# Moving the transposes and small products of a weight fold by half steps, and converting six weight tiles ahead of the loop instead of four

## The chip, the cores and the metric

The kernel runs on one core of a Trainium2 chip. The metric is the time of one execution on the device in microseconds (us). The engines are named as in the profile: PE is TensorE (PEld its weight loads), DVE is VectorE, ACT is ScalarE, POOL is GpSimd and SP is SyncE, which here only issues DMA transfers. Each engine runs its own instructions in order, so an instruction that waits holds up everything behind it on the same engine.

## The reference

Three layers follow one another, on 3072 tokens of 384 values. The first is a gated linear attention, whose state decays by alpha; the second a dense layer with the activation `h * sigmoid(h)`; the third a mixture of eight experts, of which each token takes the two with the largest noisy logits.

```
x = _attn_ref(q, k, v, alpha)            # B=4, H=8, S=768, D=48 -> 3072 x 384
h = x @ w_in                             # 384 x 2048, w_in is float64
x = (h / (1 + exp(-h))) @ w_out          # 2048 x 384, w_out is float64
logits = x @ w_gate + log1p(exp(x @ w_noise)) * noise
top2 = the two largest of 8, softmax over them
out[token] += weight * (relu(x @ w1[e]) @ w2[e])
```

The float64 weights of the dense layer matter here: `w_in` and `w_out` come as pairs of 32-bit words, which the kernel itself turns into float32, and then into a high and a low part (`win_h`, `win_l`, `wo_h`, `wo_l`) so that three passes on TensorE (high by high, high by low, low by high) give float32 accuracy.

## The kernel before

**Steps.** The tokens are cut into `NB = 8` blocks of `BT = 384`, each of three chunks of 128. For each block `j` and each of the `MF = 16` slices `m` of the hidden width there is one step, so 128 steps, numbered `i = 16 * j + m`. In a step, `l1(j, m)` multiplies a slice of `w_in` into a PSUM bank `ph` (nine matmuls, L474), `act1` makes the activation of it (`th` on ACT, `gf` on DVE, `gh` on ACT, `gl` on DVE), and `l2` (nine matmuls, L501) multiplies the result of two steps ago (`LAG = 2`) with a slice of `w_out` into the three banks `acc`. There are two `ph` banks, so `l1` of a step needs `gf` of two steps before to have read its bank. Each step also runs one `unit()` of the attention of a later chunk. Five units make a chunk: `u = 0` scans P on DVE and makes the score products (L247), `u = 1` scans R on DVE and makes the state (L264, then L272 and L273 on DVE), `u = 2` and `u = 3` make the output (L286, L290), `u = 4` transposes it into `xh` and `xl`. The first 15 units (three chunks) run ahead of the loop; this is the prologue. The other seven blocks and the experts run nothing of what is changed here.

**Weight tiles.** `w_in` and `w_out` come in 32 tiles, in the order i0, i1, i2, o0, i3, o1, i4, o2 and so on (i for `w_in`, o for `w_out`). `conv()` takes the next one: `narrow` makes float32 of it with three DVE instructions (L148 to L150) into a buffer `f` of a ring of six (named `row` and `wf`), and then the raw words of the tile three places on are requested on SP's queue, into the buffer just read. ACT makes the high part (L374). The low part of an i tile comes from a DMA on POOL's queue that adds the high part to `f` (L379) and a copy on ACT (L380), that of an o tile from DVE (L377). Of an o tile, `fold` also transposes `f` on PE (L94, three blocks, copied by ACT as `ft`, L387), and `product` multiplies that with the gate weights `wgn` (six matmuls, L394), which gives 16 more columns of `w_out` (so `l2` writes the gate logits beside its output). `product` writes into free columns of the bank of the next `l1`. ACT reads them (`fp`, L396, then `wo_h`, L397), and DVE makes the low part (L398).

**The order.** It is written out by hand. `later(n, fn)` puts a piece off by `n` ticks, and `tick()` issues what is due. In the first block (`j = 0`) each step has two halves, each with a `conv()` and a `tick()`; the first takes an i tile and the second an o tile (called halves A and B, and their tiles narrow A and narrow B, below). So on DVE a step reads: narrow A, L377 of the o tile before, pieces of the attention, `gf`, narrow B, L398, `gl`, scans of the next chunk. Within the prologue four tiles are converted.

Of the kernel before, what the change touches and what calls it, by code (L numbers as in the profile page):

```python
# [8 lines left out]
F32 = mybir.dt.float32  # L9
# [4 lines left out]
AF = mybir.ActivationFunctionType  # L14
# [7 lines left out]
DM = H * D  # L22
DFF = 2048
E = 8
# [10 lines left out]
BT = 384  # L35
# [17 lines left out]
def attention_mlp_moe(ctx: ExitStack, tc: tile.TileContext, aqk, vt, win, wout, wgn, noise, w12,  # L53
# [3 lines left out]
    PE, DVE, ACT, POOL = nc.tensor, nc.vector, nc.scalar, nc.gpsimd  # L57
# [34 lines left out]
    def flip(o, x):  # L92
        n = x.shape[0]
        PE.transpose(o, x, ident[:n, :n])  # L94
# [25 lines left out]
    wo_l = wpool.tile([128, MF, LGN], F32R)  # L120
# [7 lines left out]
    def next_f():  # L128
        turn[0] += 1
        return ring[turn[0] % len(ring)]  # L130
# [16 lines left out]
    def narrow(t, f):  # L147
        DVE.tensor_scalar(f, t[:, :, 1], 3, 0x3fffffff, op0=OP.logical_shift_left, op1=OP.bitwise_and)  # L148
        DVE.scalar_tensor_tensor(f, t[:, :, 1], -0x40000000, f, op0=OP.bitwise_and, op1=OP.bitwise_or)
        DVE.scalar_tensor_tensor(f, t[:, :, 0], 29, f, op0=OP.logical_shift_right, op1=OP.bitwise_or)  # L150
        return f.bitcast(F32)
# [156 lines left out]
    dq, lazy, clock = [], [False], [0]  # L308

    def later(n, fn, pe=0):  # L310
        dq.append((clock[0] + n, pe, fn))
# [7 lines left out]
    def tick():  # L319
        clock[0] += 1  # L320
        due = [x for x in dq if x[0] <= clock[0]]
        dq[:] = [x for x in dq if x[0] > clock[0]]
        for *_, fn in sorted(due, key=lambda x: x[1]):
            fn()
# [26 lines left out]
    def unit():  # L351
        next(gen, None)
# [6 lines left out]
    def wl(n=1):  # L359
        for _ in range(n):  # L360
            if wloads:
                kind, m = wloads.pop(0)
                (load_win if kind == "i" else load_wout)(m)

    def conv():
        if not wpreps:
            return
        kind, m = k = wpreps.pop(0)
        f = next_f()
        narrow(raw.pop(k), f.bitcast(I32))  # L370
        wl()
        h, l = (win_h, win_l) if kind == "i" else (wo_h, wo_l)
        h, l = [x[:, m].rearrange("p k j -> p (k j)") if kind == "i" else x[:, m, :DM] for x in (h, l)]
        later(1, lambda: ACT.activation(h, f, AF.Copy, scale=-1.0))  # L374
        if kind == "o":
            later(1 + (not lazy[0]), lambda: fold(m, f), 1)
            later(2, lambda: DVE.scalar_tensor_tensor(l, f, -1.0, h.bitcast(F32), op0=OP.mult, op1=OP.subtract))  # L377
        else:
            later(1, lambda: POOL.dma_start(f, h.bitcast(F32), accum_op=OP.add), 2)  # L379
            later(5, lambda: ACT.activation(l, f, AF.Copy, scale=-1.0))  # L380

    def fold(m, f):
        p = p1.tile([128, KD, 128], F32, name="ps1")
        for k in range(KD):
            flip(p[:, k], f[:, k * 128:(k + 1) * 128])
        t = stg.tile([128, KD, 128], F32, name="ft", bufs=2)
        ACT.activation(t, p, AF.Copy)  # L387

        later(1, lambda: mids.append((m, t)))

    def product(p):
        m, t = mids.pop(0)
        for k in range(KD):
            PE.matmul(p, t[:, k], wgn_t[:, k], start=(k == 0), stop=(k == KD - 1))  # L394
        h, w = wo_h[:, m, DM:], stg.tile([128, 2 * E], F32, name="fp", bufs=1)
        later(1, lambda: ACT.activation(w, p, AF.Copy, scale=-1.0))  # L396
        later(1, lambda: ACT.activation(h, w, AF.Copy))  # L397
        later(2, lambda: DVE.tensor_sub(wo_l[:, m, DM:], w, h.bitcast(F32)))  # L398

    mids = []  # L400

# [8 lines left out]
    for i in range(3 * 5):  # L410
        unit()
        tick()
        if i in (0, 1, 6, 11):
            conv()
    lazy[0] = True

# [48 lines left out]

    def l1(j, m):
        p = pl.tile([128, 512], F32, name="ph")
        if mids:
            product(p[:, BT:BT + 2 * E])
        p = p[:, :BT]  # L470
        n = 0
        for k in range(KD):
            for w, x in ((win_h, XH[j]), (win_h, XL[j]), (win_l, XH[j])):
                PE.matmul(p, w[:, m, k], x[:, k], start=(n == 0), stop=(n == 3 * KD - 1))  # L474
                n += 1
        PH[j, m] = p

    def act1(j, m):
# [189 lines left out]
    for i in range(NS + LAG):  # L668
        if i < NS:
            j, m = divmod(i, MF)  # L670
            l1(j, m)
            if MF <= i < MF + E:
                init_rows(i - MF)
# [30 lines left out]
            if j == 0:  # L704
                conv()
                tick()
                if held:
                    step(held[0])
                    step(held[0])
                conv()  # L710
                tick()
                if held:
                    run(held.pop())
            else:
                if held:
                    run(held.pop())
                    while dq:
                        tick()
                    lazy[0] = False
                run(act1(j, m))  # L720
# [5 lines left out]
        if i >= LAG:  # L726
            j, m = divmod(i - LAG, MF)
# [87 lines left out]
    for i in range(NS + LAG):  # L815
        if i < NS:
            q, f = divmod(i, FF)
# [25 lines left out]
        if i >= LAG:  # L843
            q, f = divmod(i - LAG, FF)
# [16 lines left out]
    with tc.If(bad != 0), ExitStack() as fc:  # L861
# [8 lines left out]
        with tc.For_i(0, B, 1) as b, tc.For_i(0, NP, 1) as pr:  # L870
            for s in range(2):
                av, qv, kv = [fw.tile([D, NCB, C], F32, name=f"f{x}") for x in "aqk"]
                for n, t in enumerate((av, qv, kv)):
                    o, w = (1, CP) if n == 0 else (AL + (n - 1) * NP * C, C)
# [8 lines left out]
                for x in range(2):  # L883
                    p = pl.tile([128, 512], F32, name="ph")
# [3 lines left out]
                for e in range(D):  # L888
                    u = fw.tile([D, S], F32, name="fu")
                    w = fw.tile([D, S], F32, name="fs")  # L890
                    for x in range(2):
                        h = slice(x * HS, (x + 1) * HS)
                        p = pl.tile([128, 512], F32, name="ph")
# [14 lines left out]
        for src, dst in ((win, wt[0]), (wout, wt[1])):  # L908
            for m in range(MF):
                t = fw.tile([128, DM, 2], I32, name="fraw")  # L910
                nc.sync.dma_start(t.rearrange("p n w -> p (n w)"), src[m])
                f = narrow(t, fw.tile([128, DM], I32, name="wf"))
# [6 lines left out]
        with tc.For_i(0, B, 1) as b, tc.For_i(0, NCB, 1) as c:  # L919
# [5 lines left out]
            for m in range(MF):  # L925
                p = pl.tile([128, 512], F32, name="ph")
# [9 lines left out]
            p = fps.tile([128, KD, C], F32, name="ft")  # L936
# [3 lines left out]
            p = fps.tile([128, 2 * E], F32, name="fl")  # L940
# [9 lines left out]
            for e in range(E):  # L950
                w = fw.tile([128, W3N], F32, name="fw3")
                nc.sync.dma_start(w, w12[e])
                p2 = pa.tile([128, 512], F32, name=f"acc{1 + e % 2}")
                for f in range(FF):
                    p = pl.tile([128, 512], F32, name="ph")
# [3 lines left out]
                    h = fw.tile([128, C], F32, name="fh")  # L959
# [75 lines left out]
```

## Time and profile before

| | us |
|---|---|
| three runs | 1086.50, 1091.56, 1091.65 (median 1091.56) |
| profiled execution | 1086.38 |
| its span from first to last instruction | 1084.5 |
| PE busy | 1044.5 (96%) |
| DVE busy | 591.6 (55%) |
| ACT busy | 400.7 (37%) |
| POOL busy | 225.4 (21%) |

The span is 1.9 us shorter than the execution's time; what lies around it is not in the trace. Shares of the whole span say little by themselves here, since the stages differ: PE is at work without a gap in most of the span, and in the first 140 us it is not.

### The profile page before, as it was taken

What the parts mean: (1) busy time and instruction counts of PE and PEld (TensorE: products, weight loads), DVE (VectorE), ACT (ScalarE), POOL (GpSimd) and SP (SyncE); (2) the same over time, 40 slices, a digit from 0 to 9 for tenths busy, and PEclk for the clock granted to TensorE, in tenths of its full rate; (3) what the DMA queues carried; (4) which work ended last, traced back from release to release, by engine and by line L of the source; (5) the groups of instructions that cost most, each with busy time, mean ns of one, the idle gap of its engine ahead of it and who ended that gap; (6) DMA issues with size and microseconds to landing.
All of it is one profiled execution on the core that took longest, in us unless ns stands there. A gap on an engine that the chain in (4) does not pass through costs nothing. (4 is left out here: it accounts for less than half of the span.)

```text
span 1084.5 us, 16739 instructions
## 1 busy us (share of the span) xinstructions
PE 1044.5 (96%) x6323; PEld 1012.1 (93%) x6323; DVE 591.6 (55%) x1369; ACT 400.7 (37%) x869; POOL 225.4 (21%) x223
## 2 busy tenths in 40 slices
PE   5987799999999999999999999999999999999997
PEld 4877799999999999999999998999999999999997
DVE  6787956657778687775737552244333333324221
ACT  3344443334333433334344332244333333323221
POOL 4121201310313003130010132211212122221203
PEclk9988899999999999999999999999999999999999
DMA  8465661445424324240033342445444344353204
GB/s 222 124 164 169 154 204 60 133 148 186 123 78 145 100 79 129 85 138 18 1 103 108 117 139 30 114 106 155 112 96 118 86 95 107 68 121 77 47 10 54
DMA packets 53577, 117.16 MB, mean 108 GB/s; under 512 B 6768, under 2 KB 31856, under 8 KB 53488
## 3 DMA queue, kind: packets, MB, share of 16 engines
q1 hardware_dynamic: 39312, 90.99, 28.0%
q0 software_dynamic: 13760, 24.43, 12.3%
q8 instruction: 52, 0.85, 0.3%
q10 hardware_dynamic: 416, 0.58, 0.2%
q14 instruction: 37, 0.30, 0.1%
HBM read 82.22 MB, written 30.61 MB: 104 GB/s over the span
## 5 line engine op out<-in xcount | busy, mean ns | idle before, releaser
L784 PE MATMUL acc<-w3h,hx 128*128 128x384 f32 x832 | 241.1, 341 | 1.2 <-ACT y L794 1.2
L765 DVE SCALAR_TENSOR_TENSOR hx<-ph,hx 128x64 fp32r<-128x64 f32 (+1 forms) x192 | 79.1, 442 | 293.2 <-ACT hx L761 293.2
L796 POOL DMA_INDIRECT out_dram<-y,xrow x64 | 100.6, 1572 | 335.3 <-ACT y L794 291.7
L761 ACT ACTIVATE hx<-ph 128x448 fp32r<-128x448 f32 (+1 forms) x128 | 65.4, 517 | 267.9 <-PE ph L758 190.6
L784 PEld LDWEIGHTS acc<-w3h,hx 128*128 128x128 f32 x832 | 152.7, 188 | 4.8 <-ACT y L794 1.6
L784 PE MATMUL acc<-w3l,hx 128*128 128x384 f32 x448 | 149.9, 335 | 0.0
L501 PE MATMUL acc<-wo_h,gh 128*128 128x400 f32 x384 | 142.5, 371 | 0.0
L758 PE MATMUL ph<-xh,w3h 128*128 128x384 f32 (+1 forms) x384 | 135.2, 352 | 0.0
L758 PE MATMUL ph<-xh,w3l 128*128 128x384 f32 (+1 forms) x384 | 134.7, 351 | 0.0
L758 PE MATMUL ph<-xl,w3h 128*128 128x384 f32 (+1 forms) x384 | 134.4, 350 | 0.0
L501 PE MATMUL acc<-wo_l,gh 128*128 128x400 f32 x384 | 133.1, 347 | 0.0
L501 PE MATMUL acc<-wo_h,gl 128*128 128x400 f32 x384 | 133.0, 346 | 0.0
L474 PE MATMUL ph<-xh,win_h 128*128 128x384 f32 x384 | 132.7, 345 | 0.0
L474 PE MATMUL ph<-xh,win_l 128*128 128x384 f32 x384 | 130.7, 340 | 0.0
L474 PE MATMUL ph<-xl,win_h 128*128 128x384 f32 x384 | 130.6, 340 | 0.0
L491 DVE TENSOR_TENSOR gl<-gf,gh 128x384 fp32r<-128x384 f32 x128 | 83.0, 649 | 72.4 <-ACT gh L489 71.7
L481 ACT ACTIVATE th<-ph 128x384 f32<-128x384 f32 x128 | 62.5, 488 | 151.3 <-PE ph L474 149.5
L489 ACT ACTIVATE gh<-gf 128x384 fp32r<-128x384 f32 x128 | 66.9, 523 | 110.7 <-DVE gf L484 110.7
L484 DVE SCALAR_TENSOR_TENSOR gf<-th,ph 128x384 f32<-128x384 f32 x128 | 70.4, 550 | 65.2 <-ACT th L481 64.3
L784 PEld LDWEIGHTS acc<-w3l,hx 128*128 128x128 f32 x448 | 80.8, 180 | 0.7
L501 PEld LDWEIGHTS acc<-wo_h,gh 128*128 128x128 f32 x384 | 73.2, 191 | 2.5
L758 PEld LDWEIGHTS ph<-xh,w3l 128*128 128x128 f32 x384 | 72.1, 188 | 3.5
(153 smaller groups left out, 1707.8 us busy)
## 6 DMA issues: line engine op xcount, KB each, us to landing
wraw<-in_w_dram SPq DMA_DIRECT2D x64, 384.0 KB, 4.2
aqk<-in_aqk_dram SPq DMA_DIRECT2D x23, 674.2 KB, 5.5
wraw<-in_win_dram SPq DMA_DIRECT2D x32, 384.0 KB, 3.5
wraw<-in_wout_dram SPq DMA_DIRECT2D x32, 384.0 KB, 3.2
xrow<-xd SPq DMA_DIRECT2D x45, 196.5 KB, 3.8
xd<-pad SPq DMA_DIRECT2D x8, 589.5 KB, 7.0
v<-in_v_dram SPq DMA_DIRECT2D x24, 192.0 KB, 5.8
wf<-win_h POOLq DMA_DIRECT2D x15, 192.0 KB, 3.8
```

The source lines that it names most:

```text
L474: PE.matmul(p, w[:, m, k], x[:, k], start=(n == 0), stop=(n == 3 * KD - 1))
L481: ACT.activation(th, p, AF.Tanh, scale=-0.5)
L484: DVE.scalar_tensor_tensor(g, th, 1.0, p, op0=OP.add, op1=OP.mult)
L489: ACT.activation(gh, g, AF.Copy)
L491: DVE.tensor_tensor(gl, g, gh.bitcast(F32), OP.subtract)
L501: PE.matmul(ACC[j][i], g[:, sl], w[:, m], start=(m == 0 and n == 0), stop=(m == MF - 1 and n == 2))
L758: PE.matmul(p[:, :N], w[:, k, fs], x[:, k], start=(n == 0), stop=(n == 3 * KD - 1))
L761: ACT.activation(hx[:, :N], p[:, :N], AF.Relu)
L765: DVE.scalar_tensor_tensor(hx[:, o:o + b - a], p[:, a:b], 0.0, hx[:, a:b].bitcast(F32), op0=OP.max, op1=OP.subtract)
L784: PE.matmul(AC3[e, g][t][:m], hx[:, o:o + m], w[:, f], start=(f == 0 and q == 0), stop=(f == FF - 1 and q == len(prods) - 1))
L796: st = POOL.indirect_dma_start(out=out, out_offset=bass.IndirectOffsetOnAxis(ap=xr[:n, RW - 1:].bitcast(I32), axis=0), in_=y[a:a + n], in_ ...
```

## The change

Four edits. In the loop `fold` comes two ticks after its tile's `narrow` instead of one (in the prologue it was two already). `product` is issued behind the nine matmuls of `l1` instead of ahead of them, in the same bank. What reads it comes one tick later on ACT and two ticks later on DVE. And two more tiles (six instead of four) are converted in the prologue, after its units 8 and 13, so that every tile of the loop comes one step earlier.

```
-            later(1 + (not lazy[0]), lambda: fold(m, f), 1)
+            later(2, lambda: fold(m, f), 1)
...
-        later(1, lambda: ACT.activation(w, p, AF.Copy, scale=-1.0))
-        later(1, lambda: ACT.activation(h, w, AF.Copy))
-        later(2, lambda: DVE.tensor_sub(wo_l[:, m, DM:], w, h.bitcast(F32)))
+        later(2, lambda: ACT.activation(w, p, AF.Copy, scale=-1.0))
+        later(2, lambda: ACT.activation(h, w, AF.Copy))
+        later(4, lambda: DVE.tensor_sub(wo_l[:, m, DM:], w, h.bitcast(F32)))
...
-        if i in (0, 1, 6, 11):
+        if i in (0, 1, 6, 8, 11, 13):
             conv()
...
     def l1(j, m):
         p = pl.tile([128, 512], F32, name="ph")
-        if mids:
-            product(p[:, BT:BT + 2 * E])
-        p = p[:, :BT]
+        q, p = p[:, BT:BT + 2 * E], p[:, :BT]
         n = 0
         for k in range(KD):
             for w, x in ((win_h, XH[j]), (win_h, XL[j]), (win_l, XH[j])):
                 PE.matmul(p, w[:, m, k], x[:, k], start=(n == 0), stop=(n == 3 * KD - 1))
                 n += 1
+        if mids:
+            product(q)
         PH[j, m] = p
```

What this does to the engines' orders is seen on three of them. On PE, at the third `l1` of the loop (step 2), the rows were these; `ft` is a transposed tile, `row` the tile that `narrow` B of this step has just written, `ps1` the bank of the transposes.

```order
L394 MATMUL ph_528<-wgn_t_145,ft_443 128x16 x3
L474 MATMUL ph_528<-xh_240,win_h_111 128x384
...
L474 MATMUL ph_528<-xh_240,win_l_112 128x384
L94 MATMUL ps1_569<-ident_94,row_115 128x128 x3
L286 MATMUL ps1_576<-S_369,aqk_248 128x96
```

Now they are these (the changed file has the matmuls of `l1` on line 472).

```order
L472 MATMUL ph_549<-xh_240,win_h_111 128x384
...
L472 MATMUL ph_549<-xh_240,win_l_112 128x384
L394 MATMUL ph_549<-wgn_t_145,ft_519 128x16 x3
L94 MATMUL ps1_575<-ident_94,row_115 128x128 x3
L286 MATMUL ps1_597<-S_382,aqk_248 128x96
```

The small product stands behind `l1`. The transposes stand at the same place, but `row` is now the tile that `narrow` B wrote in the step before.

On ACT, one whole step (the third of the loop) was this; `wf3` and `row` are ring buffers, `gh_559` belongs to the activation of the step before.

```order
L380 ACTIVATE win_l_112<-wf3_116 128x384
L396 ACTIVATE fp_532<-ph_528 128x16
L397 ACTIVATE wo_h_113<-fp_532 128x16
L374 ACTIVATE win_h_111<-wf3_116 128x384
L489 ACTIVATE gh_559<-gf_557 128x384
L374 ACTIVATE wo_h_113<-row_115 128x384
L387 ACTIVATE ft_573<-ps1_569 128x384
L481 ACTIVATE th_583<-ph_528 128x384
```

Now it is this.

```order
L380 ACTIVATE win_l_112<-wf3_116 128x384
L374 ACTIVATE win_h_111<-wf3_116 128x384
L387 ACTIVATE ft_579<-ps1_575 128x384
L489 ACTIVATE gh_584<-gf_582 128x384
L396 ACTIVATE fp_562<-ph_549 128x16
L397 ACTIVATE wo_h_113<-fp_562 128x16
L374 ACTIVATE wo_h_113<-row_115 128x384
L481 ACTIVATE th_604<-ph_549 128x384
```

The copy `ft` of the transposes now stands ahead of `gh`, and the two reads of the product (L396, L397) behind it.

On DVE, at the end of the third chunk in the prologue, the rows were these; L230 is the last piece of the next chunk's preparation, L306 makes the low part `xl` on which the loop's first `l1` waits.

```order
L148 TENSOR_SCALAR row_115<-wraw_205 128x384
L149 SCALAR_TENSOR_TENSOR row_115<-wraw_205,row_115 128x384
L150 SCALAR_TENSOR_TENSOR row_115<-wraw_205,row_115 128x384
L230 TENSOR_TENSOR aqk_248<-aqk_248,R_331 112x512
L377 SCALAR_TENSOR_TENSOR wo_l_114<-row_115,wo_h_113 128x384
L306 TENSOR_TENSOR xl_241<-ps1_403,xh_240 128x3x128
```

Now they are these.

```order
L230 TENSOR_TENSOR aqk_248<-aqk_248,R_337 112x512
L148 TENSOR_SCALAR row_115<-wraw_300 128x384
L149 SCALAR_TENSOR_TENSOR row_115<-wraw_300,row_115 128x384
L150 SCALAR_TENSOR_TENSOR row_115<-wraw_300,row_115 128x384
L306 TENSOR_TENSOR xl_241<-ps1_415,xh_240 128x3x128
```

A `narrow` has come between L230 and L306, and the same has happened one chunk earlier.

## Rows read from the trace of the kernel before

**Rows 1.** Busy time in stretches; per engine busy us (instructions), granted PE clock.

```profile
core 0: us, PE busy (x) PEld busy (x) DVE busy (x) ACT busy (x) POOL busy (x), PEclk, DMA share, GB/s
240.00:400.00 160.00, 160.00 (x1067) 157.20 (x1067) 118.06 (x298) 61.44 (x139) 27.47 (x33) 1.00 0.41 123
...
46.10:135.76 89.66, 72.33 (x430) 67.91 (x431) 76.23 (x154) 40.41 (x110) 16.93 (x20) 0.89 0.61 164
135.76:155.81 20.05, 20.05 (x125) 19.89 (x124) 9.75 (x22) 9.24 (x27) 1.06 (x1) 0.91 0.63 195
```

**Rows 2.** PE in order of time: start, length, what, [idle before <-releaser].

```profile
90.62 0.52 PE L94 MATMUL ps<-ident,row 128*128 128x128 f32 x3 [1.26 <-DVE wo_l L398]
...
99.52 0.87 PE L94 MATMUL ps<-ident,row 128*128 128x128 f32 x3 [3.67 <-DVE wo_l L398]
...
130.06 0.88 PE L94 MATMUL ps<-ident,row 128*128 128x128 f32 x3 [4.60 <-DVE wo_l L398]
```

**Rows 3.** DVE in order of time, around two of these waits.

```profile
134.22 0.35 DVE L148 TENSOR_SCALAR row<-wraw 128x384 int32<-128x384 int32 x1
...
135.20 0.56 DVE L150 SCALAR_TENSOR_TENSOR row<-wraw,row 128x384 int32<-128x384 int32 x1
138.60 0.18 DVE L398 TENSOR_TENSOR wo_l<-fp,wo_h 128x16 fp32r<-128x16 f32 x1 [2.84 <-ACT wo_h L397]
139.43 0.56 DVE L491 TENSOR_TENSOR gl<-gf,gh 128x384 fp32r<-128x384 f32 x1 [0.65 <-ACT gh L489]
```

**Rows 4.** What DVE waited for from 46.10 to 135.76: us, times, longest.

```profile
DVE wo_l L398 <- ACT wo_h L397: 6.6, 3, 4.6
DVE gl L491 <- ACT gh L489: 4.2, 7, 0.7
```

**Rows 5.** The end of the first `l1` on PE, then ACT in order of time.

```profile
48.86 0.52 PE L474 MATMUL ph<-xh,win_l 128*128 128x384 f32 x1
...
49.42 0.18 ACT L396 ACTIVATE fp<-ph 128x16 f32<-128x16 f32 x1 [3.80 <-PE ph L474]
...
107.92 0.18 ACT L396 ACTIVATE fp<-ph 128x16 f32<-128x16 f32 x1 [6.21 <-PE ph L474]
```

**Rows 6.** What PE waited for from 46.10 to 155.81.

```profile
PE ps L94 <- DVE wo_l L398: 12.8, 7, 4.6
PE ps L94 <- DVE row L150: 4.4, 2, 3.7
```

**Rows 7.** PE from step 13 to the start of step 16.

```profile
141.88 0.74 PE L394 MATMUL ph<-wgn_t,ft 128*128 128x16 f32 x6
142.47 0.42 PE L474 MATMUL ph<-xh,win_h 128*128 128x384 f32 x1
...
144.12 0.49 PE L94 MATMUL ps<-ident,wf 128*128 128x128 f32 x3
144.45 0.49 PE L94 MATMUL ps<-ident,row 128*128 128x128 f32 x3
...
155.81 0.74 PE L394 MATMUL ph<-wgn_t,ft 128*128 128x16 f32 x6
```

**Rows 8.** The prologue's third chunk: PE, and DVE's two waits.

```profile
43.41 0.87 PE L94 MATMUL ps<-ident,row 128*128 128x128 f32 x3
44.19 0.90 PE L94 MATMUL ps<-ident,xr 128*128 128x128 f32 x3
...
46.15 0.67 PE L474 MATMUL ph<-xh,win_h 128*128 128x384 f32 x1
...
34.15 0.56 DVE L306 TENSOR_TENSOR xl<-ps,xh 128x384 fp32r<-128x384 f32 x1 [2.88 <-ACT xh L305]
...
45.65 0.56 DVE L306 TENSOR_TENSOR xl<-ps,xh 128x384 fp32r<-128x384 f32 x1 [2.35 <-ACT xh L305]
```

**Rows 9.** Stretches after the long waits of PE, columns as in the first group.

```profile
99.50:105.00 5.50, 5.48 (x22) 5.48 (x23) 4.14 (x9) 1.72 (x4) 0.00 (x0) 0.50 0.50 151
130.00:139.00 9.00, 8.94 (x33) 8.84 (x34) 5.65 (x13) 2.59 (x8) 0.00 (x0) 0.50 0.56 156
```

## The prediction

> **What bounds the kernel now.** I read the stretches of busy time first. From 240 to 400 us PE is busy for the whole 160 us [rows 1], so there only fewer matmuls would help. From 46.10, where the first `l1` is about to start, to 135.76, where `narrow` B of step 12 ends, PE is busy 72.33 of 89.66 us at a granted clock of 0.89, and DVE 76.23 [rows 1]. That stretch is 13 steps, each with two `narrow`. From there to 155.81, the start of step 16, PE is busy all the time [rows 1].
>
> Next I read who waits. From 46.10 to 155.81 PE waits 12.8 and 4.4 us, always at the transposes of `fold` (L94) and always for DVE [rows 6]; the long waits are 3.67 and 4.60 us, the shorter ones like 1.26 [rows 2]. DVE itself waits 6.6 us for the high part of the small product (L397 on ACT) and 4.2 us for `gh`, together 10.8 [rows 4]. And ACT holds that up: its read `fp` starts at 49.42, right after the last matmul of `l1` in the same bank ends (48.86 + 0.52 = 49.38), and at 107.92 it has stood still for 6.21 us [rows 5]. So there is a ring: PE's transposes wait for `narrow` B of the same step, the next `l1` stands behind them on PE, `fp` waits on ACT for that `l1`, L398 on DVE waits for `fp`, and behind L398 stand `gl` and the next `narrow`. The two engines take turns although neither is full.
>
> **The change, part by part.**
>
> The transposes a step later. `narrow` B of the step before has long been done when PE comes to them: between the two lie the rest of that step on PE and a whole `l1`. All 17.2 us of PE's waiting at L94 [rows 6] lose their reason. PE is then held only where `l1` needs `gf` of two steps ago (two banks) and where a unit needs a result of DVE; both come earlier in DVE's step than `narrow` B. What is late next is DVE: it never gets a pause from PE, and its work is the longer one. Without its named waits DVE needs 89.66 - 10.8 = 78.9 us for the 13 steps, 6.1 a step. PE needs 72.33 / 13 = 5.6, of which 14.5 us ran at half clock [rows 1, 9]; at the full one it is (72.33 - 7.25) / 13 = 5.0. So DVE is the bound.
>
> The product behind `l1`, and read later. Its work on PE is the same. `fp` no longer stands ahead of `gh`, and L398 comes a step after its product, so the 6.6 us of DVE's waiting for L397 [rows 4] go. Its user `l2` comes one step after L398, as before, since every tile is one step earlier. Queued behind `fp` on ACT are now L397, the high part of the o tile and `th`; `th` is needed by DVE only after the next `narrow` A.
>
> `ft` ahead of `gh` on ACT. This is the added wait: `gh` now stands behind the copy of transposes that stand behind `l1` and the product on PE. Where PE is ahead it costs nothing; its cover is the 1.5 us of `narrow` B between `gf` and `gl` on DVE (134.22 to 135.76 [rows 3]), in which `gh` is made. From below nothing, then; from above the wait of 0.65 us [rows 3] in each of 13 or 14 steps, 9.1. I take 4.2, what the waits for `gh` cost now [rows 4], since light steps of DVE (no scans) are shorter than PE's, and there PE will still be the later one.
>
> Two tiles in the prologue. Their DVE work is two `narrow` of 1.5 us. Both come right ahead of L306, which waits 2.88 and 2.35 us for ACT's `xh` [rows 8], so both are covered; uncovered they would cost 3.1. On PE the transposes of o0 move from 43.41, where PE would have had to wait for the copy `xr` anyway, to the middle of the third chunk, where PE runs without a pause: 0.78 us later (43.41 to 44.19 [rows 8]). The product no longer stands between `xr`'s transposes and the first `l1` (44.19 + 0.90 to 46.15), but `l1` also needs `xl`, which is made from 45.65 on [rows 8], so only about 0.4 comes back. Net 0.4 us lost. The raw words of two more tiles are asked for on SP's queue ahead of chunk 4, which is put off by one `narrow`, under 2 us; DVE scans chunk 4 only in step 0, after 46.10, and the request comes before the 34.15 of [rows 8], so 12 us lie between. Their other ACT, POOL and DMA work is moved, not added.
>
> What the earlier tiles buy comes at the end. Today 20.05 us pass from the end of `narrow` B of step 12 to the start of step 16, with two more tiles in step 13 [rows 1]. Then step 12 has the last ones. Step 13 on PE may begin when `gf` of step 11 is done, that is before `narrow` B, 1.5 us ahead of the end. From the start of step 13 to that of step 16 PE takes 155.81 - 141.88 = 13.93 us now, with two sets of transposes in step 13; one of them (144.12 to 144.45, 0.33 us [rows 7]) falls into step 12. 13.93 - 0.33 - 1.5 = 12.1 us.
>
> **The sum.** Before, 46.10 to 155.81 is 109.7 us. After: DVE's work 78.9, its waits for `gh` 4.2, the prologue 0.4, the end 12.1: 95.6. Gain 14.1. From step 16 on PE has no gap (bar the experts' end, which is untouched), so all of it reaches the end: 1086.38 - 14.1 = **1072 us**, on the level of the profiled execution. Of the three runs one lies there (1086.50), two lie 5.1 higher, for a reason that no trace here shows; I forecast the lower level and let the range hold the upper one. With no wait for `gh` left it is 1068, with 9.1 it is 1077.
>
> **Rivals.**
>
> *`gh` comes late in every step.* Product (0.74) and transposes (0.49, [rows 7]) stand between the end of `l1` and `ft`, in place of two short reads (`fp` 0.18, [rows 5]). If PE isn't ahead of DVE, each step loses about 1.0 us, 13 in all, and with the waits gone for L397 and the shorter end the gain is 18.3 - 13 = 5: 1081 us. For it: the granted clock was 0.50 for 5.5 and 9.0 us after PE's long waits [rows 9], and a slow PE is not ahead. Against it: 5.6 against 6.1 us a step.
>
> *`th` waits for the product.* The bank of `l1` is PE's until the last matmul into it: `fp` started only 0.04 us after the end of `l1`, though its own columns had been done since 46.15 [rows 5, 8]. If that holds for `th` too, it now starts after the product, 0.59 us later (141.88 to 142.47 [rows 7]); on the path in all 13 steps that is 7.7 us, 1080 us. Against it: `th` is the last of its step on ACT, behind copies that wait for `narrow` B. The Trainium skill (PSUM — Partial Sum Buffer, section "PSUM bank collisions raise a hardware error") says that two engines must not touch one bank at the same time and that the semaphores should guard whole banks; by that rule it is this rival's delay that each step pays, and the trace agrees with the rule, 49.42 against 49.38.
>
> *The ring closes elsewhere.* PE, let go at L94, is held by the next thing that DVE owes it (`am` before L264, `gf` before `l1`), DVE keeps its 10.8 us of waits under other names, and PE is as late at the end as now: 1083 to 1086 us, no change to tell. For it: DVE is busy 85% of the stretch already [rows 1].
>
> *Slower: one long wait in each step.* PE's waits come together in front of one instruction, and each one is followed by half clock. After 3.67 and 4.60 us the same transposes took 0.87 and 0.88 us, after 1.26 they took 0.52 [rows 2], and the granted clock of 0.50 over 14.5 us [rows 9] cost half of it, 3.6 us each time. With that in each of 13 steps PE would need about 5.0 + 3.6 a step, 112 us, and 12.1 behind it: 124 against 109.7, 1101 us. It turns into a loss only when more than 8 of 13 steps are slow (a step may take (109.7 - 12.5) / 13 = 7.5 us, 2.5 over 5.0). Against it: what remains to be waited for is 6.1 - 5.0 = 1.1 us a step on average, long only where scans and masks meet, in two of five steps. The Trainium skill (TensorE: Matmul & The Clock Gate, section "Part 1: The HAM clock gate") says that the clock follows how busy the engine has been, and lies at 1.2 GHz when it was idle; the rows agree, half of 2.4 GHz after the long waits.
>
> **Chances.** The forecast 0.61, `gh` late 0.14, `th` behind the product 0.07, the ring elsewhere 0.10, slower 0.08. A measurement of this kernel tells about 0.5% from no change, 5.4 us, so faster is 0.82, the same 0.10, slower 0.08. The range reaches from 1066 (no wait left, and less half clock) to 1084 (both rivals in between, and the upper level of the forecast, 1077, with some of the waits): it leaves out the slower case, most of the ring and little else.
>
> **What would show it.** Right: no wait of PE at L94 for DVE in the loop's first block; no wait of DVE at L398; the first `l1` still at about 46.5; step 16 starts near 142; DVE busy over 90% from step 0 to 12; the longest wait of PE is at L264 or at the first matmul of `l1`, for `am` or `gf`. Wrong: waits of DVE at `gl` that grow beyond 0.7 us, waits at `gf` for `th`, long stretches of granted clock 0.50 in most steps, or a first `l1` later than 48.

## The result, and the profile after

| | before | after |
|---|---|---|
| median of the runs, us | 1090.23 (1086.50 to 1091.65, 4 runs) | 1073.55 (1072.28 to 1073.80, 4 runs) |
| profiled execution, us | 1086.38 | 1072.28 |
| its span, us | 1084.5 | 1070.4 |
| PE busy, us | 1044.5 | 1036.6 |
| mean granted PE clock | 0.988 | 0.996 |

The ratio is 0.985 with a 95% interval of 0.9822 to 0.9878: faster, by 16.7 us between the medians and by 14.1 between the profiled executions, to whose level the forecast (1072, a gain of 14.1) belongs. Executions of one kernel differ by some us: all of the kernel before lie between 1086.06 and 1092.01. The spans differ by 14.1 us, and so do the starts of the first big matmul of step 16 (156.40 before, 142.28 after): all of this gain is made in the first block, and all of it reaches the end.

What each engine waited for, in the changed kernel, from the first `l1` to the start of step 16 (us, times, longest); first DVE, then PE. They answer to [rows 4] and [rows 6].

```profile
DVE gl L491 <- ACT gh L489: 6.4, 3, 5.4
...
DVE gf L484 <- ACT th L481: 2.9, 3, 2.2
...
PE ph L472 <- DVE gf L484: 2.9, 3, 1.9
PE ps L94 <- DVE wf L150: 2.8, 1, 2.8
PE ps L247 <- ACT ft L387: 1.9, 2, 1.3
PE ps L94 <- DVE wo_l L398: 1.2, 2, 0.7
PE ps L264 <- DVE am L253: 0.9, 1, 0.9
```

PE's 17.2 us at the transposes have become 4.0, and DVE waits for the product's high part (L397) no more. What PE is held by instead is short and spread: `gf`, `ft`, `am`. The exception is one wait of 2.8 at L94, and DVE's one of 5.4 at `gl`; they belong together, and to the end of the block, as the stretches show (columns as in [rows 1]).

```profile
46.43:124.55 78.12, 68.34 (x462) 65.35 (x463) 75.19 (x156) 44.20 (x117) 16.27 (x20) 0.99 0.71 195
124.55:142.28 17.73, 17.73 (x104) 17.70 (x104) 6.59 (x17) 7.04 (x21) 0.00 (x0) 0.87 0.51 157
122.20:129.00 6.80, 6.78 (x26) 6.75 (x27) 4.50 (x11) 3.40 (x9) 0.00 (x0) 0.51 0.00 0
```

The first is the one of 13 converting steps (124.55 is the end of `narrow` B of step 12, the last tile): 78.1 us where it was 89.7, with DVE busy 96% of it instead of 85%. The second, from there to step 16, is 17.7 us, where it was 20.05. The third lies across both, and PE ran it at half clock. PE in order of time shows why.

```profile
118.86 0.52 PE L94 MATMUL ps<-ident,row 128*128 128x128 f32 x3 [0.66 <-DVE wo_l L398]
...
122.22 0.81 PE L94 MATMUL ps<-ident,wf 128*128 128x128 f32 x3 [2.84 <-DVE wf L150]
122.82 0.58 PE L286 MATMUL ps<-S,aqk 112*128 112x96 f32 x2
...
128.38 0.52 PE L472 MATMUL ph<-xh,win_h 128*128 128x384 f32 x1
```

In step 12 there are two sets of transposes: those of o13 (`row`), written a step ago, and those of o14 (`wf`). The i tiles are used up by then, so an o tile stands in the first half of the step; two ticks later is the second half of the same step, and its transposes wait for the `narrow` A just ahead of them, as before the change all of them waited for the `narrow` of their own step. DVE shows why that `narrow` was late.

```profile
115.64 1.90 DVE L148 TENSOR_SCALAR row<-wraw 128x384 int32<-128x384 int32 x1
...
119.19 1.23 DVE L219 TENSOR_TENSOR_SCAN R<-aqk,past 112x516 f32<-112x516 f32 x1
...
121.61 0.56 DVE L150 SCALAR_TENSOR_TENSOR wf<-wraw,wf 128x384 int32<-128x384 int32 x1
```

One instruction of `narrow` B of step 11 took 1.90 us instead of 0.35 (POOL multiplied two tiles of the attention at the same time, from 115.01 on). The rest of `narrow` B, L398, `gl` and the scan R of the chunk came next, and only then `narrow` A. DVE's wait of 5.4 us at `gl` lies behind all this: ACT's `ft` waited 4.72 us for the next transposes on the slow PE, until 131.47, and `gh` stands behind `ft`.

### The profile page after: what moved, and what is told of

The parts are those of the page before. It is cut to its first block, busy times and chain, and to the rows that moved or that the text cites. A ratio compares the mean times of both kernels' runs of the same rounds, so it can differ in the third digit from the quotient of the medians.

```text
span 1070.4 us, 16732 instructions
## 1 busy us (share of the span) xinstructions
PE 1036.6 (97%) x6323; PEld 1005.4 (94%) x6323; DVE 589.3 (55%) x1369; ACT 402.7 (38%) x869; POOL 224.6 (21%) x223
## 5 line engine op out<-in xcount | busy, mean ns | idle before, releaser
L472 PEld LDWEIGHTS ph<-xh,win_h 128*128 128x128 f32 x384 | 72.7, 189 | 5.1 <-DVE gf L484 4.0
```

## The experiments

Each was timed beside runs of the kernel before; the gain is the difference of the medians. The span and the start of step 17 (both us) belong to one execution each, and executions of one kernel differ by up to 7 us, so a few us in these columns count only where the medians say the same. Of the kernel before, the traced execution is one of the shortest, so gains read from the spans come out smaller. The theory is called "ring" below: PE's transposes, the next `l1`, ACT's read of the product, DVE's L398 and the next `narrow` wait for one another in a circle.

| | ratio to before (95%) | median us | gain us | span us | step 17 starts |
|---|---|---|---|---|---|
| before | 1 | 1088.1 | | 1084.5 | 161.4 |
| tiles alone | 1.0013 (0.9995 to 1.0030) | 1089.27 | -1.2 | 1085.5 | 162.3 |
| read alone | 0.9910 (0.9884 to 0.9937) | 1078.02 | 10.1 | 1075.2 | 151.8 |
| transposes alone | 0.9829 (0.9804 to 0.9854) | 1069.75 | 18.4 | 1069.5 | 145.0 |
| read and tiles | 0.9904 (0.9880 to 0.9929) | 1077.83 | 10.3 | 1076.8 | 153.7 |
| transposes and tiles | 0.9873 (0.9841 to 0.9904) | 1073.84 | 13.9 | 1072.1 | 148.7 |
| transposes and read | 0.9805 (0.9781 to 0.9829) | 1067.73 | 20.0 | 1067.2 | 143.7 |
| the change, again | 0.9849 (0.9830 to 0.9869) | 1072.23 | 15.9 | 1071.4 | 148.3 |

**Transposes alone.** On the kernel before:

```
-            later(1 + (not lazy[0]), lambda: fold(m, f), 1)
+            later(2, lambda: fold(m, f), 1)
```

> Only the transposes come a step later; product, its reads and the four tiles are as before. Theory 'ring' (PE's wait at L94 for narrow B of the same step holds up the next l1, and through it ACT and DVE): PE's 17.2 us of waiting at L94 go almost whole, DVE's 6.6 us at L398 shrink to under 3 since l1 comes earlier, and the kernel is 8 to 11 us faster. Theory 'tiles' (the gain is the conversion work taken out of the loop): at most 3 us. Theory 'read' (ACT's read of the product ahead of gh is the cause): at most 3 us, with the waits at L398 as before.

15.0 us less in the span, more than the 8 to 11 expected, and no less than the whole change. PE's waits at L94 fell from 17.2 to 1.7 us, and DVE's at L398, up to the end of `narrow` B of step 12, from 6.6 to 0.8, as the theory has it. That the tiles or the later read are needed for the gain is refuted. Up to step 16 ACT still waited for `l1` at `fp`:

```profile
ACT fp L396 <- PE ph L474: 17.7, 10, 3.8
```

17.7 us instead of 47.4 in the kernel before; DVE's waits at L398 were 4.4 us there instead of 13.0. So ACT's long waits at `fp` were for the most part PE's waiting at L94, handed on.

**Tiles alone.** On the kernel before:

```
-        if i in (0, 1, 6, 11):
+        if i in (0, 1, 6, 8, 11, 13):
```

> Only the two tiles more in the prologue. Theory 'ring': the waits of PE at L94 stay at about 1.2 us a step, the loop has one converting step less (6.9 us become 4.5), so 2 to 4 us faster. Theory 'tiles': 9 us or more.

No gain at all; the 2 to 4 us of my own theory didn't come either. From the start of step 3 to that of step 16 it took 84.0 us instead of 87.5. But from step 0 to step 3 it took 26.8 instead of 22.8. PE's row in step 2 and the stretch behind it show what went on:

```profile
66.64 0.87 PE L94 MATMUL ps<-ident,row 128*128 128x128 f32 x3 [4.47 <-DVE wo_l L398]
...
66.60:73.50 6.90, 6.86 (x31) 6.86 (x31) 4.16 (x9) 1.74 (x4) 0.00 (x0) 0.54 0.73 197
```

A wait of 4.47 us, and half clock for 6.9 us behind it. The kernel before has three waits of more than 3 us at L94, in steps 1, 7 and 11 (3.71, 3.67 and 4.60 us); here they are in steps 2, 7 and 11 (4.47, 3.72 and 4.59). With the ring intact, two tiles more ahead of the loop shift which step the first long wait falls into, and it costs as much there.

**Read alone.** On the kernel before, with four tiles; DVE's read is put off by one tick and not by two, so that it is still ahead of its `l2`.

```
-        later(1, lambda: ACT.activation(w, p, AF.Copy, scale=-1.0))
-        later(1, lambda: ACT.activation(h, w, AF.Copy))
-        later(2, lambda: DVE.tensor_sub(wo_l[:, m, DM:], w, h.bitcast(F32)))
+        later(2, lambda: ACT.activation(w, p, AF.Copy, scale=-1.0))
+        later(2, lambda: ACT.activation(h, w, AF.Copy))
+        later(3, lambda: DVE.tensor_sub(wo_l[:, m, DM:], w, h.bitcast(F32)))
...
-        if mids:
-            product(p[:, BT:BT + 2 * E])
...
+        if mids:
+            product(q)
```

> Only the product behind l1 and read one tick later on ACT; DVE reads it one tick later, not two, so that with four tiles it is still ahead of its l2. Theory 'ring': PE still waits at L94 for 12 us or more, DVE's 6.6 us at L398 go, and the kernel is 1 to 5 us faster. Theory 'read': 8 us or more.

9.3 us less in the span: above the 1 to 5 expected of the ring, and as much as "read" expected (8 or more). PE's waits at L94 fell to 9.9 us (five, the longest 3.4), below the 12 that "ring" expected, although nothing was done to the transposes. Both edits work on the same circle: 15.0 alone and 9.3 alone give 17.3 together, not 24 (18.4, 10.1 and 20.0 by the medians).

**The transposes put back** in the changed kernel (the first diff, reversed).

> The change with the transposes put back behind narrow B of their own step. Theory 'ring': PE waits at L94 for more than 10 us again, and of the gain of 14 to 16 us 4 to 7 are left. Theories 'tiles' and 'read': 10 us or more are left.

PE waits 10.5 us at L94 again, as "ring" expected. Of the gain 7.7 us are left by the spans and 10.3 by the medians: the first is just above the 4 to 7 of "ring", the second just inside the "10 or more" of "read". So the time doesn't part the two theories; it is what the read alone gives (9.3 and 10.1).

**Four tiles** in the changed kernel (the tiles' diff reversed, and `later(3, ...)` for DVE's read, as above).

> The change with four tiles in the prologue (and the product read by DVE one tick later than before, not two, so that it is ahead of its l2). Theory 'ring': 9 to 12 us of the gain are left, and l1 of step 0 starts within 0.5 us of where it did. Theory 'tiles': under 5 us are left.

Not 9 to 12 us are left but 17.3 by the spans and 20.0 by the medians: it is faster than the changed kernel (0.9805 against 0.985, intervals 0.9781 to 0.9829 and 0.9822 to 0.9878, which overlap at their ends; 0.9830 to 0.9869 in its second measurement, which doesn't). Step 0 starts at 46.3 and 46.4, so the prologue isn't it. In all four pairs that differ by the tiles (in two of them also by the tick of DVE's read), the kernel with six has the longer span: by 1.0, 1.6, 2.6 and 3.2 us. By the medians it is so in three (1.2, 4.1 and 4.5); with the read alone the two are level (0.2 the other way).

**The product put back ahead of `l1`** in the changed kernel, read as before.

> The change with the product ahead of l1 again and read as before. Theory 'ring': with PE let go at L94, fp seldom waits for long, and 10 us or more of the gain are left; ACT waits for l1 at fp again. Theory 'read': under 6 us are left.

12.4 us are left by the spans and 13.9 by the medians, as "ring" expected, and ACT waits 25.4 us for `l1` at `fp` again. The wait for o14's transposes is here too (2.93 us). So the move of the product, once the transposes are moved, is worth 1.7 us of the span with six tiles and 2.3 with four, 1.6 and 2.0 by the medians: less than executions of one kernel differ by.

**The last transposes later.** The changed kernel, with those of o14 a tick later still:

```
-            later(2, lambda: fold(m, f), 1)
+            later(2 + (len(wpreps) == 1), lambda: fold(m, f), 1)
```

> The change, with the transposes of the last tile but one (o14, an o tile in the first half of its step) a tick later still. In the changed kernel PE waits 2.84 us for them in step 12, and then runs 6 us at half clock. If this is what makes the end 17.7 us long instead of the 12.1 forecast, it gets 3 to 6 us shorter, and the kernel as much faster than the changed one (1068 to 1070 us). If PE is held there by something else anyway, no difference.

1067.82 us, ratio 0.9805 (0.9780 to 0.9830), span 1066.0, step 17 at 142.6: the shortest span of the study. The granted clock of its stretches to step 16:

```profile
46.30:124.50 78.20, 72.67 (x475) 69.44 (x476) 74.85 (x154) 44.05 (x117) 16.25 (x20) 1.00 0.74 195
124.50:137.70 13.20, 13.20 (x91) 13.20 (x90) 7.01 (x18) 6.82 (x21) 0.00 (x0) 1.00 0.70 220
```

`narrow` B of step 12 ends at 125.14 here, and from there to the start of step 16 (137.72) it takes 12.6 us, where the changed kernel took 17.7 and the forecast had 12.1. The half clock of step 12 is gone. That of the start is not, though the column says 1.00:

```profile
56.70 0.52 PE L472 MATMUL ph<-xl,win_h 128*128 128x384 f32 x1
57.02 0.52 PE L472 MATMUL ph<-xh,win_l 128*128 128x384 f32 x1
...
59.60 0.33 PE L472 MATMUL ph<-xl,win_h 128*128 128x384 f32 x1
59.77 0.34 PE L472 MATMUL ph<-xh,win_l 128*128 128x384 f32 x1
```

Up to 57.02, in steps 0 and 1, these matmuls start 0.32 us apart and take 0.52, as the one at 128.38 in the stretch of granted clock 0.51 above; in step 2 they start 0.17 us apart. In every kernel here the first `l1` runs so.

**PE kept at work during the wait.** The changed kernel, with 24 transposes of a constant ahead of those of o14, whose results are overwritten:

```
+        if m == 14:
+            for _ in range(8):
+                for k in range(KD):
+                    flip(p[:, k], ident)
```

> The changed kernel with 24 more transposes of a constant, about 2.7 us of PE at full clock, right ahead of o14's transposes, into the bank that these then overwrite; PE has work while it would wait. Theory 'half clock': the wait itself costs 2.8 us and the half clock behind it another 3.4 (6.8 us at 0.51); with PE kept at work the granted clock stays near 1.00 in step 12, step 12 is about 3 us shorter, and the kernel 2 to 4 us faster although it does more. Theory 'wait only': no difference, or slower by what the transposes overrun.

```profile
119.02 2.78 PE L94 MATMUL ps<-ident 128*128 128x128 f32 x24
122.03 0.55 PE L94 MATMUL ps<-ident,wf 128*128 128x128 f32 x3 [0.22 <-DVE wf L150]
...
114.00:130.00 16.00, 14.66 (x108) 14.02 (x107) 13.18 (x26) 7.67 (x22) 2.86 (x3) 1.00 0.32 91
```

The same data are waited for until the same moment (122.03 and 122.22), but the granted clock stays at 1.00, and step 12 takes 9.8 us (115.6 to 125.4) instead of 12.6 (115.8 to 128.4). The kernel is 1068.86 us against 1072.23 of the changed one in the same job, and its span 1067.0 against 1071.4, although PE does 2.8 us of useless work. So of the 5.2 us that o14's transposes cost step 12 (12.6 against the 7.4 of the kernel that has them later), 2.8 are the half clock and the rest the wait. The Trainium skill (TensorE: Matmul & The Clock Gate, section "A second HAM failure mode: psum-queue depth-cycling") says of another kernel that frequent short pauses between groups of matmuls made the clock fall and rise again and that this cost throughput. The trace agrees in that much: pauses of 0.66 and 2.84 us, a clock of 0.51 behind them, 2.8 us lost.

**Eight tiles, with the last transposes later**, and without.

```
-        if i in (0, 1, 6, 8, 11, 13):
+        if i in (0, 1, 6, 8, 9, 11, 13, 14):
```

> The change with eight tiles in the prologue. If DVE bounds the converting steps, each step less saves a DVE step of 6.0 us less the PE step of 4.5 that remains, 1 to 3 us, unless the prologue gets longer: its first l1 then starts later by up to 3 us (two narrow uncovered), and nothing is won.

> Eight tiles in the prologue and the transposes of o14 a tick later. Theory 'the wait at o14's transposes is a cost of its own': with it gone the eight tiles gain as six did, 2 to 4 us against eight tiles without it (1068.75). Theory 'the tiles in the prologue are worth their DVE steps': faster than six tiles with the same edit by 1 to 3 us. If the prologue's own growth (first l1 at 47.5 instead of 46.3) eats it: the same as six, 1067 to 1069 us.

1068.75 us without and 1068.64 with, ratios 0.9813 (0.9789 to 0.9838) and 0.9827 (0.9804 to 0.9850). Step 0 starts at 47.5 and 47.6, 1.1 us later than with six. Neither beats six tiles with the last transposes later. In the trace of the first, o14's transposes still wait 2.38 us, now in step 11. In the profiled execution of the second, which took 1072.23 us, step 12 began after a wait of 2.00 us for `gf` and then ran 10.5 us at half clock, without the wait at the transposes. That the tiles are worth their steps is not shown, and that the wait at the transposes is the only thing that brings the clock down there is refuted.

**The product ahead of `l1`, with the last transposes later.**

> Six tiles, the transposes a step later and those of o14 a tick later still, but the product ahead of l1 and read as before. Theory 'two links of one ring, either is enough': the move of the product adds little once the transposes are moved, and this is within 2 us of the same with the product moved (1067.8). Theory 'each link has its own price': 4 us or more slower than that.

1067.89 us (1067.10 to 1073.67), ratio 0.9823 (0.9795 to 0.9851): by the median within 0.1 us of the kernel with the product moved. Its trace is of an execution of 1073.12 us (span 1071.3): there step 3 took 9.9 us at a granted clock of 0.52, where the kernel without the late transposes took 6.9 at 0.78. That the move of the product adds little once the transposes are moved stands; whether 2 us or nothing, these times don't tell. That either link is enough doesn't: the read alone gives half of what both give (10.1 of 20.0).

**The change again**, beside these three.

> The changed kernel once more, beside the other three on one chip: 1072 to 1074 us, so that differences of 3 us can be told.

1072.23 us (1071.25 to 1073.21). With the last transposes later, or with four tiles, the kernel is 4 to 5 us faster than this, by medians that were not taken side by side.

## Why the prediction was right, and where two of its terms were not

**The mechanism was right.** PE waited at the transposes for `narrow` B of the same step, and ACT and DVE behind it; moved by a step, these waits are gone but for 4.0 us. Alone, that edit gives as much as the whole change. How much the moved product gives by itself (9.3 us) the prediction didn't see.

**The bound was right.** The forecast took DVE's work without waits, 78.9 us, as the length of the converting steps. They took 78.1. The reading behind it, that PE needs less, holds with more room: the prediction counted 14.5 us of half clock and left out what followed the first long wait (3.71 us, step 1); a mean of 0.89 over 89.66 us, its own row, makes about 20 us of it.

**The waits for `gh`, taken as 4.2 us, are none** in those steps: DVE's only named waits between 46.43 and 124.55 are 1.1 us for `xh`, at the start, and 0.4 for `th`. `gh` is made under `narrow` B, the cover that the prediction named; the lower end of that bound held. The rival of a late `gh` is wrong with it, and so is that of `th` behind the product (0.4 us). Where PE was slow, at the end, `gh` did come late behind `ft`, by 5.4 us, far over the 0.7 that the prediction had named as a sign of being wrong; PE was busy all that time, so it isn't a loss of its own.

**The end, taken as 12.1 us, is 17.7.** The step that failed is "Then step 12 has the last ones", with the sentence that the second set of transposes falls into step 12. It does, and I counted its 0.33 us on PE, but not what it waits for: of an o tile in the first half, two ticks later is the same step. That wait of 2.84 us and the half clock behind it are 5.1 of the 5.6 us: the late transposes bring the end to 12.6. The wait is also why "no wait of PE at L94" and "the longest wait of PE is at L264 or at the first matmul of `l1`" didn't come true. The two errors, 5.0 too long in the steps (83.1 against 78.1) and 5.6 too short in the end, cancel, and the prologue's 0.4 is 0.3 (46.43 against 46.15). That the sum of 95.6 fits (78.1, 17.7 and 0.3 make 96.1) is luck in that much.

**What the tiles buy** was put at the end's shortening. It isn't: with four tiles and the other two edits step 16 starts at 138.2, 4 us earlier than with six. The tiles moved o14 into a step whose `narrow` A comes behind a scan and a slowed instruction; that this is the reason for all of the 4 us is not shown. With o14 mended, six tiles and four can't be told apart (1067.82 and 1067.73).

**The slower rival** has its mechanism in the trace, once: a wait and half clock in step 12. It named 8 of 13 steps as the point from which it decides.

## What to carry to other kernels

Where several in-order engines wait for one another in a circle, look for the link with the least reason to be where it is; moving it by a step frees the others, and a second edit on the same circle adds less than it gives alone (here some 2 us instead of 10). When a piece is put off by a fixed number of ticks, check the places where the pattern ends: there the same number can put it next to what it waits for. Count a wait of PE with the half clock that can come behind it, here 2.8 us for a wait of 2.8. Compare medians before believing a difference of two traces.

## What was not expected of the hardware

The clock fell after a wait of 2.84 us that followed one of 0.66 by three transposes, and after one of 2.00 us in the kernel with eight tiles; in the kernel before, a wait of 1.26 left it up. Waits of nearly the same length differ: ahead of step 3, one of 1.87 us in the changed kernel left it at 1.00 over the step, while one of 1.95 with the transposes and tiles and one of 1.96 with the product ahead of `l1` and the last transposes later were followed by 0.78 and 0.52.

How long PE is slow at the start differs between two executions of the changed kernel: in the first trace its matmuls run at full rate from 53.03 on, in that of "the change, again" only from 62.01 on, and from step 0 to step 3 it took 18.3 and 20.6 us. What decides it stays open. Of the kernel before, the executions of 1089.05 us and more, where the clock is on record, have a mean granted clock of 0.981 to 0.986, the shorter ones one of 0.987 to 0.989; so its upper level goes with more half clock, but no trace of it shows where.

A `narrow` instruction takes longer while POOL multiplies. In the traces of the kernel before, the changed one and the one with the last transposes later, all those that took over 0.7 us (0.81 to 2.88, alone 0.35 and 0.56) lie beside such a product, and before the change the wait of 4.60 us at L94 came right behind the one of 2.88.

ACT waits 17.2 us for the product's buffer in the changed kernel, which has one `fp` that DVE's L398 must have read:

```profile
ACT fp L396 <- DVE wo_l L398: 17.2, 12, 2.6
```

That it costs nothing is argued, not tested: L398 stands right behind `narrow` B on DVE, and the next piece of ACT's work but one (L374) waits for `narrow` B anyway. No run has a second buffer.
